# An extra GpSimd addition behind each scatter, and TensorE products in four column groups

## The chip, the cores and the metric

The kernel runs on one core of a Trainium2 chip. A core has five engines with instruction streams of their own: TensorE (PE in the profile; its weight loads are PEld), VectorE (DVE), ScalarE (ACT), GpSimd (POOL) and SyncE (SP, which here only issues DMAs); a q behind the name (SPq) is that engine's sequencer. They meet through semaphores. TensorE writes to PSUM, a memory of eight banks of 2 KB per partition; VectorE and ScalarE read it from there. The metric is the device time of one execution in microseconds, of which the median of several runs is taken. The profiled execution is one more, and all rows below are from it.

## The reference

All inputs are float32. Attention with `B, H, S, D = 2, 8, 768, 64` in which a query sees only keys of its own cluster, then an ELU feed-forward layer, then a routed mixture of experts:

```python
q_assign = np.argmax(np.einsum('bhsd,hcd->bhsc', q_n, c_n), axis=-1)   # 16 centroids a head
k_assign = np.argmax(np.einsum('bhsd,hcd->bhsc', k_n, c_n), axis=-1)
mask = q_assign[:, :, :, None] == k_assign[:, :, None, :]
scores = np.where(mask, scale * np.matmul(q, k.transpose(0, 1, 3, 2)), -1e9)
attn_out = softmax(scores) @ v
x = attn_out.transpose(0, 2, 1, 3).reshape(B * S, H * D)               # 1536 x 512
h = x @ w_in; g = np.where(h > 0, h, np.exp(np.minimum(h, 0)) - 1)     # 512 -> 2048
x = g @ w_out                                                          # 2048 -> 512
do_compute = x @ w_skip > 0                                            # a token is skipped or routed
logits = x @ w_gate; e_idx = argmax(logits); gate_w = softmax(logits)[e_idx]   # 8 experts
out = x + where(do_compute, gate_w * (relu(x @ w1[e_idx]) @ w2[e_idx]), 0)     # 512 -> 1024 -> 512
```

## The kernel before

The two batches are treated differently. Batch 0 is "dense": four units n = 0 to 3, each a pair of heads, compute all 768 x 768 scores of each head with the mask folded into the product as extra rows. Batch 1 is "sorted": for the pairs j = 0 to 3 (`NSORT = 4`) the rows of q, k and v are written to DRAM in the order of their cluster, and only pieces of rows that can share a cluster are multiplied.

**Order.** Inside the attention and the feed-forward layer no scheduler orders anything: `ORDER` (L49) is one flat list of steps, written out by hand, each `name:n`. The steps are issued one after the other, each step sends its instructions to the engines that it uses, and every engine works through its own part of the list in that order. The routing of the last block has a list of its own, `TAIL` (L35), in which `h` steps are products of the feed-forward layer, `T` turns a token tile, `L` takes its gate logits, `C` chooses, `R` ranks, `F` fills, `x` fetches.

**Dense unit.** `turn`, `turn_head` and `turn_rest` (L349 to L377) transpose q and k and split them into a high and a low part in float32r (a form of float32 that TensorE multiplies in one pass), kept as `T[n][nm, "H"]` and `["L"]`. Then the clusters: `similar` (L399) multiplies the centroids with q and k; per half of 384 tokens there are three float32r products (high x high, high x low, low x high) for q and three for k, which fill partitions 0 to 63 of a PSUM bank through the zero-padded weights `cwH` and `cwL`; `similar_out` (L403) copies a half to SBUF, and `turn_back` (L408) makes six transposes of 64 x 128, so that tokens lie on partitions. `largest` (L425), `less_largest` (L429, on GpSimd), `candidates`, `first_of_them` and `one_hot` make the argmax one-hot, `turn_one_hot` and `mask_rows` make mask rows of it, and `move` (L463, SyncE) puts rows into place by DMA. `v_rest` (L490, GpSimd) splits v. Then for twelve pieces s of each unit: `scores` (L498), `peak` (L504, VectorE), `expo` (L511, ScalarE), `flip` (L519, three TensorE transposes a half into PSUM), `head` (L531, ScalarE copies the transposed half to float32r), `rest` (L537, VectorE subtracts that copy), `pv`, `pv_low`, `pv_sum` (L550 to L567, products with v).

**Sorting, spread among the dense units' steps.** For pair j: `sort_turn` and `sort_raw` (L703, L708) transpose q and k of batch 1; `sort_similar` (L716) makes twelve float32 products with the 32 columns of `cwF` as the moving side, which land with tokens on partitions. `sort_max` to `sort_index` (L755) compute each token's row, `idx`. `sort_zero` (L688, L689) clears the DRAM buffers with DMAs of SyncE. `sort_scatter` (L770) sends one indirect DMA from GpSimd for each pair j, chunk c of 128 tokens and r (q or k and v, of head 0 or 1):

```python
store = self.nc.gpsimd.indirect_dma_start(
    dst[2 * j + h], bass.IndirectOffsetOnAxis(ap=self.idx[:, j, 4 * c + r:4 * c + r + 1], axis=0),
    self.sort_rows(j, c // 3)[:, c % 3, lo:hi], None, bounds_check=1023, oob_is_err=False)
```

That is 24 for each pair and 96 in all (steps `sc0a` to `sc5d`). They stand in the list alone between other engines' steps, so on GpSimd they mostly follow each other.

**Sorted rows.** `rows_load` (L794) reads the sorted rows back, two heads of a pair at a time, and `rows_turn` to `rows_divide` (L801 to L856; L836 is the transpose) do attention on 16 pieces. `gather` (L868) fetches results in token order with 48 indirect DMAs of GpSimd, which stand among the rounding steps of the weights (`round64`, L1202 to L1223; its last operation, L1223, is a GpSimd addition) and `w_low` (L1249, GpSimd).

**Feed-forward and routing.** `ffn_h` (L1269) and `ffn_second` or `second_ops` (L1308, L1325) multiply in two blocks of 768 tokens, 16 steps of 128 columns each. Routing takes 12 token tiles: `route` turns a tile (L1445), makes four float32 products of the turned tile with 16 columns of gate weights `wgs` (L1453), copies the logits (L1455), then `choose` (from L1457). For the first block this stands beside the second block's feed-forward (`route_beside`), for the last in `TAIL`. Then each of eight experts computes its tokens (L1675 to L1768).

Of the kernel before, what the change touches and what calls it, by code (L numbers as in the profile page):

```python
# [10 lines left out]
F32 = mybir.dt.float32  # L11
F32R = mybir.dt.float32r
# [22 lines left out]
TAIL = ("h3 h3 h3 T0 T2 h3 L0 T1 h5 L2 L1 T3 h5 C0 h4 h4 R0 h4 h4 x- T4 h5 L3 L4 C3 h5 x0 T5 R3 x2 L5 x4 F0 C5 R5 N5 x3 x1 x5 F5 F3").split()  # L35
# [22 lines left out]
    simq1:1 exp5:0 rest3b:0 simk1:1 peak6:0 head4a:0 sT1:1 flip4b:0 rest4a:0 scores7a:0 suk1:0 loadv:0 head4b:0 flip5a:0
    scores7b:0 sek1:0 back:1 exp6:0 rest4b:0 sv:1 flip5b:0 peak7:0 sload0:1 scores8a:0 mx:1 scores8b:0 head5a:0 ssim0:0 eqsub:1
    ssim1:0 pv1a:0 rest5a:0 pv1c:0 peak8:0 pv1b:0 flip6a:0 pv1d:0 head5b:0 exp7:0 scores9b:0 first:1 exp8:0 rest5b:0 scores10a:0  # L60
    least:1 smx:0 vtH:1 flip6b:0 sone:0 head6a:0 pvlow1:0 scum:0 srank:0 pvsum1:0 pv2a:0 rest6a:0 flip7a:0 pv2c:0 equal:1 pv2b:0
    head7a:0 vtL:1 pv2d:0 moveT0:1 scores9a:0 sidx:0 rows:1 head6b:0 rest6b:0 flip7b:0 sc2c:0 rest7a:0 pvlow2:0 peak9:0 oT:1
    flip8a:0 loadqk:1 head7b:0 pvsum2:0 rest7b:0 exp9:0 scores10b:0 turnq0:2 peak10:0 pv3a:0 pv3b:0 pv3c:0 scores11b:0 sc3b:0
    scores11a:0 sc4b:0 THq0:2 TLq0:2 flip8b:0 turnq1:2 sc0d:0 head8a:0 sc5a:0 rest8a:0 exp10:0 moveO0:1 flip9a:0 head8b:0
    scores0a:1 peak11:0 THq1:2 head9a:0 scores0b:1 rest8b:0 pv3d:0 TLq1:2 flip9b:0 rest9a:0 exp11:0 turnk0:2 flip10a:0 head9b:0
    rest9b:0 pvlow3:0 pvsum3:0 scores1b:1 scores1a:1 head10a:0 flip10b:0 sc0a:0 pv4a:0 rest10a:0 flip11a:0 THk0:2 peak0:1
    sload1:1 sc3a:0 TLk0:2 pv4b:0 pv4c:0 head10b:0 rest10b:0 head11a:0 exp0:1 pv4d:0 suq0:1 seq0:1 flip11b:0 scores2a:1 sc2d:0
    sc1b:0 pvlow4:0 rest11a:0 flip0a:1 turnk1:2 peak1:1 pvsum4:0 head11b:0 THk1:2 exp1:1 rest11b:0 TLk1:2 scores2b:1 pv5a:0
    peak2:1 invert:0 head0a:1 pv5b:0 flip0b:1 suq1:1 zero:1 pv5c:0 scores3a:1 seq1:1 sc4d:0 scores3b:1 simq0:2 head0b:1 rest0a:1
    exp2:1 sc2a:0 simk0:2 sc1a:0 flip1a:1 rest0b:1 peak3:1 flip1b:1 scores4a:1 sT0:2 head1a:1 scores4b:1 rest1a:1 moveT1:1  # L70
    suk0:1 exp3:1 sc5b:0 pv5d:0 flip2a:1 sc1c:0 peak4:1 moveO1:1 sek0:1 loadv:3 head1b:1 scores5a:1 sc5c:0 simq1:2 sc0b:0 smem:0
    simk1:2 head2a:1 exp4:1 rest1b:1 scores5b:1 flip2b:1 scores6b:1 sT1:2 head2b:1 rest2a:1 loadv:1 pvlow5:0 suk1:1 flip3a:1
    peak5:1 scores6a:1 rest2b:1 sc1d:0 sek1:1 flip3b:1 back:2 sumT:0 exp5:1 scores7a:1 pvsum5:0 sc2b:0 head3a:1 peak6:1 rest3a:1
# [91 lines left out]
class _Core:  # L165
# [26 lines left out]
    def first_loads(self):  # L192
# [1778 lines left out]
```

## Time and profile before

| | us |
|---|---|
| median of three runs (747.60 to 751.81) | 749.87 |
| the profiled execution | 748.56 |
| its span, first to last instruction | 746.8 |
| TensorE busy (85% of the span) | 635.4 |
| VectorE busy (58%) | 431.6 |
| ScalarE busy (53%) | 392.9 |
| GpSimd busy (36%) | 271.7 |

Busy shares are means over a span in which several stages follow each other: the dense units until about 260 us, then the sorted rows, the feed-forward layer until about 605 us, routing and experts. "remote" as the releaser of a wait means that the trace shows no instruction of this core whose end set the semaphore just then; the chain of waits calls the same thing "another core or an unknown queue". A `<-issue` is time in which an engine waited for nothing that the trace shows.

### The profile page before, as it was taken

What the parts mean: (1) busy time and instruction counts of PE and PEld (TensorE: products, weight loads), DVE (VectorE), ACT (ScalarE), POOL (GpSimd) and SP (SyncE); (2) the same over time, 40 slices, a digit from 0 to 9 for tenths busy, and PEclk for the clock granted to TensorE, in tenths of its full rate; (3) what the DMA queues carried; (4) which work ended last, traced back from release to release, by engine and by line L of the source; (5) the groups of instructions that cost most, each with busy time, mean ns of one, the idle gap of its engine ahead of it and who ended that gap; (6) DMA issues with size and microseconds to landing.
All of it is one profiled execution on the core that took longest, in us unless ns stands there. A gap on an engine that the chain in (4) does not pass through costs nothing.

```text
span 746.8 us, 11604 instructions
## 1 busy us (share of the span) xinstructions
PE 635.4 (85%) x3988; PEld 576.0 (77%) x3988; DVE 431.6 (58%) x982; ACT 392.9 (53%) x850; POOL 271.7 (36%) x289
## 2 busy tenths in 40 slices
PE   5991892874772399999999999999999999999996
PEld 3881882773662399888989889999998988999995
DVE  6680790872660398999698775333245545135663
ACT  4761770852641398776776765544544622124552
POOL 3247067047057302865664352323223203121101
PEclk9795896897695599999999999999999999999999
DMA  7877064576331039666654553642421027989960
GB/s 174 208 172 195 14 156 112 129 159 165 91 90 37 22 101 251 183 178 199 204 180 154 165 161 101 254 169 61 165 57 57 14 110 266 384 291 319 335 231 18
DMA packets 99957, 118.30 MB, mean 158 GB/s; under 512 B 47553, under 2 KB 68209, under 8 KB 99888
## 3 DMA queue, kind: packets, MB, share of 16 engines
q1 hardware_dynamic: 92080, 106.70, 47.4%
q0 software_dynamic: 6096, 10.34, 4.3%
q8 instruction: 33, 0.54, 0.3%
q10 hardware_dynamic: 1712, 0.43, 0.3%
q14 instruction: 36, 0.29, 0.1%
HBM read 80.17 MB, written 27.80 MB: 145 GB/s over the span
## 4 chain that ended last, share of the span: by engine, by line
PE 65%; DVE 11%; another core or an unknown queue 11%; ACT 6%; issue 3%; DMA 1%; SPq 0%; POOL 0%; POOLq 0%; ACTq 0%; DVEq 0%
PE ps_p L1269 7%; PE ps_v L1269 6%; PE ps_t L1720 5%; PE ps_t L519 4%; PE ps_p L1735 4%; PE ps_v L1735 4%; PE ps_v L550 4%; PE ps_sB L1308 3%; PE ps_sA L1308 3%; PE ps_t L1308 3%; PE ps_sA L498 2%; PE ps_sB L498 2%; PE ps_sA L1325 2%; DVE cv_b L1217 1%
## 5 line engine op out<-in xcount | busy, mean ns | idle before, releaser
L519 PE MATMUL ps_t<-ident,pe 128*128 128x128 f32 x288 | 53.5, 307 | 59.9 <-issue 30.4
L519 PEld LDWEIGHTS ps_t<-ident,pe 128*128 128x128 f32 x288 | 38.6, 159 | 66.8 <-issue 32.8
L531 ACT ACTIVATE ptH<-ps_t 128x384 fp32r<-128x384 f32 x96 | 46.0, 491 | 82.5 <-remote 59.0
L537 DVE TENSOR_TENSOR ptL<-ps_t,ptH 128x384 fp32r<-128x384 f32 x96 | 52.1, 551 | 58.9 <-ACT ptH L531 45.7
L868 POOL DMA_INDIRECT og<-od,idx x48 | 51.2, 1066 | 55.2 <-ACT rp L830 27.8
L1223 POOL TENSOR_TENSOR r<-cv_b,cv_t 128x512 int32<-128x512 int32 x32 | 42.9, 1341 | 47.5 <-DVE cv_b L1217 19.7
L550 PE MATMUL ps_v<-ptH,vt 128*128 128x256 f32 x144 | 44.0, 328 | 14.6 <-issue 8.6
L1269 PE MATMUL ps_p<-xH,w1H 128*128 128x384 f32 x128 | 44.3, 346 | 1.9 <-DVE gL L1297 1.5
L1768 POOL DMA_INDIRECT out_dram<-o,dest x10 | 11.0, 1104 | 93.4 <-DVE o L1766 92.8
L1293 DVE SCALAR_TENSOR_TENSOR ps_p<-e,ps_p 128x384 f32<-128x384 f32 x32 | 17.9, 560 | 45.1 <-ACT e L1291 45.1
L550 PEld LDWEIGHTS ps_v<-ptH,vt 128*128 128x128 f32 x144 | 30.7, 215 | 16.6 <-issue 9.3
L1269 PE MATMUL ps_v<-xH,w1H 128*128 128x384 f32 x124 | 42.0, 339 | 1.3 <-DVE gL L1297 1.3
L1269 PE MATMUL ps_p<-xL,w1H 128*128 128x384 f32 x128 | 43.0, 336 | 0.0
L550 PE MATMUL ps_v<-ptL,vt 128*128 128x256 f32 x144 | 41.5, 312 | 0.3 <-DVE ptL L537 0.3
L1269 PE MATMUL ps_v<-xL,w1H 128*128 128x384 f32 x124 | 41.6, 335 | 0.0
L1249 POOL TENSOR_TENSOR w2L<-r,w2H 128x512 fp32r<-128x512 f32 x12 | 15.3, 1279 | 71.5 <-PE ps_t L1308 57.4
L1289 ACT ACTIVATE e<-ps_p 128x384 f32<-128x384 f32 x32 | 15.7, 490 | 40.7 <-PE ps_p L1269 40.7
L770 POOL DMA_INDIRECT kvs<-rowsH,idx x24 | 23.8, 990 | 33.8 <-DVE idx L755 23.1
L1735 PE MATMUL ps_p<-xs,ew 128*128 128x128 f32 (+2 forms) x256 | 35.4, 280 | 0.5 <-ACT xs L1683 0.5
L1735 PEld LDWEIGHTS ps_p<-xs,ew 128*128 128x128 f32 x256 | 33.7, 191 | 2.3 <-ACT xs L1683 0.6
L1735 PEld LDWEIGHTS ps_v<-xs,ew 128*128 128x128 f32 x256 | 33.7, 191 | 1.8
L1735 PE MATMUL ps_v<-xs,ew 128*128 128x128 f32 (+2 forms) x256 | 35.0, 279 | 0.0
(491 smaller groups left out, 2006.7 us busy)
## 6 DMA issues: line engine op xcount, KB each, us to landing
ew<-in_moe_w_dram SPq DMA_DIRECT2D x32, 1024.0 KB
d<-in_moe_w_in_dram SPq DMA_DIRECT2D x16, 512.0 KB
d<-in_moe_w_out_dram SPq DMA_DIRECT2D x16, 512.0 KB
wf_d<-r SPq DMA_DIRECT2D x16, 512.0 KB
r<-wf_d SPq DMA_DIRECT2D x16, 512.0 KB
zk<-kvs SPq DMA_DIRECT2D x8, 520.0 KB
KA<-kH SPq DMA_DIRECT2D x16, 192.0 KB
kvs<-zeros SPq DMA_DIRECT2D x8, 325.0 KB
```

Of the source, the lines that this page charges most:

```text
L498: self.nc.tensor.matmul(self.sc[u][:, half, 0:384], lhsT=d["Q" + a][0:rows, c * 128:c * 128 + 128], rhs=d["K" + a][0:rows, half * 384:half ...
L519: self.nc.tensor.transpose(ps[:, 0, j * 128:j * 128 + 128], self.pe[u][:, half, j * 128:j * 128 + 128], self.ident)
L531: self.nc.scalar.activation(self.split(u, half)[0], self.tp[u, half][:, 0, 0:384].rearrange("p (c q) -> p c q", c=3), AF.Copy)
L537: self.nc.vector.tensor_tensor(l, self.tp.pop((u, half))[:, 0, 0:384].rearrange("p (c q) -> p c q", c=3), h.bitcast(F32), ALU.subtract)
L550: self.nc.tensor.matmul(self.vp[n, j], lhsT=self.vt[n][:, j // NG, c, :], rhs=t, start=(part == 0 and i == 0), stop=(part == 3 and i == 2 ...
L770: store = self.nc.gpsimd.indirect_dma_start(dst[2 * j + h], bass.IndirectOffsetOnAxis(ap=self.idx[:, j, 4 * c + r:4 * c + r + 1], axis=0), ...
L868: self.nc.gpsimd.indirect_dma_start(self.og[j][:, c, h, :], None, self.o_d[i], bass.IndirectOffsetOnAxis(ap=self.idx[:, j, 4 * c + h:4 * c ...
L1223: G.tensor_tensor(r[:, j * 512:j * 512 + 512].bitcast(I32), b, self.cvt.pop((f, j)), ALU.add)
L1269: self.nc.tensor.matmul(ps, lhsT=w[:, c, :], rhs=x[:, c, :], start=(i == 0), stop=(i == 11))
L1308: self.nc.tensor.matmul(self.y[bl][part][t], lhsT=a[:, t * 128:t * 128 + 128], rhs=w, start=(f == 0 and i == 0), stop=(f == NF - 1 and i = ...
L1720: PE.matmul(y[0][0:W], lhsT=a, rhs=b, start=(f == 0 and i == 0), stop=(f == NF - 1 and i == 2))
L1735: PE.matmul(ps[:, 0:W], lhsT=w1[:, c, i * 128:i * 128 + 128], rhs=xs[:, c, 0:W], start=(c == 0), stop=(c == 3))
```

## The change

There are five parts. Behind each of the 96 scatters GpSimd adds a tile `idle` of 128 x 96 elements to itself; nothing reads the tile otherwise.

The centroid products of a dense unit are now four products of 384 columns in float32, (half 0, half 1) x (q, k), each with the 32 columns of `cwF` as weights and each writing its own 32 partitions of one PSUM bank; the high and the low part of q and k are multiplied one after the other and summed, so there are eight instructions in the code. One copy of 128 x 384 and three transposes of 128 x 128 follow. `cwH` and `cwL` are gone. The sorted pairs get the same form, four float32 products, a copy (`sTT`) and three transposes (`sback`). Since the columns come out in another order, the index tile is addressed through `group` and `index`.

The gate logits are four products in the same manner: for each 128 of the 512 features the 32 columns of weights stay and the tile's 128 tokens move, into 32 partitions of their own; a copy, one transpose and a sum over the four parts follow, done just after the next tile's products (`back`), or by `B` in `TAIL`. The tile that stands alone (`nt == 1`) keeps the old form.

`second_ops` names its operands through indices; the instructions are the same. `ORDER` is written anew: 1890 steps in place of 1902. The scatters stand at much the same places among the dense steps, the fills `zero:2` and `zero:3` stand 14 and 20 exponentials earlier, `bload1` and `bload2` earlier too. `TAIL` has `B0` and `B3`, with `h5` and `h4` steps ahead of `B0`.

```diff
@@ -32,7 +32,8 @@
-TAIL = ("h3 h3 h3 T0 T2 h3 L0 T1 h5 L2 L1 T3 h5 C0 h4 h4 R0 h4 h4 x- T4 h5 L3 L4 C3 h5 x0 T5 R3 x2 L5 x4 F0 C5 R5 N5 x3 x1 x5 F5 F3").split()
+TAIL = ("h3 h3 h3 T0 T2 h3 L0 T1 h5 L2 h5 L1 T3 h4 B0 C0 h4 h4 h4 x- R0 T4 h5 L3 h5 L4 x0 B3 C3 T5 x2 L5 R3 x4 "
+        "F0 C5 R5 N5 x3 x1 x5 F5 F3").split()
@@ -47,119 +48,118 @@
 ORDER = """
-    turnq0:0 THq0:0 turnq1:0 TLq0:0 THq1:0 turnk0:0 TLq1:0 THk0:0 turnk1:0 TLk0:0 THk1:0 TLk1:0 simq0:0 simk0:0 loadqk:0 sT0:0
...
+    turnq0:0 THq0:0 turnq1:0 TLq0:0 THq1:0 turnk0:0 TLq1:0 THk0:0 turnk1:0 TLk0:0 THk1:0 TLk1:0 loadqk:0 sim:0 sT:0 back:0 sv:0
+    mx:0 eqsub:0 turnq0:1 rawq0:1 first:0 THq0:1 turnq1:1 TLq0:1 least:0 rawq1:1 THq1:1 equal:0 TLq1:1 rows:0 moveT0:0 moveO0:0
...
@@ -390,22 +384,23 @@
-    def similar(self, n, nm, half):
-
-        p, cs, o = n % (self.H // 2), slice(half * 384, half * 384 + 384), 32 if nm == "q" else 0
-        if nm == "q":
-            self.sim[n, half] = self.bank_p()
-        for j, (w, x) in enumerate(((self.cwH, "H"), (self.cwH, "L"), (self.cwL, "H"))):
-            self.nc.tensor.matmul(self.sim[n, half][0:64, 0:384], lhsT=w[:, p, o:o + 64], rhs=self.T[n][nm, x][:, cs],
-                                  start=(nm == "q" and j == 0), stop=(nm == "k" and j == 2))
-
-    def similar_out(self, n, half):
-        self.nc.scalar.activation(self.rows[0:64, half * 384:half * 384 + 384], self.sim.pop((n, half))[0:64, 0:384], AF.Copy)
+    def similar(self, n):
+
+        ps, p, T = self.bank_p(), n % (self.H // 2), self.T[n]
+        self.sim[n] = ps
+        for x in "HL":
+            for i, (half, nm) in enumerate(itertools.product(range(2), "qk")):
+                self.nc.tensor.matmul(ps[32 * i:32 * i + 32, 0:384], lhsT=self.cwF[:, p, :],
+                                      rhs=T[nm, x][:, half * 384:half * 384 + 384].bitcast(F32), start=(x == "H"), stop=(x == "L"))
+
+    def similar_out(self, n):
+        self.simT = self.sort_tile("sT", [128, 384], F32)
+        self.nc.scalar.activation(self.simT, self.sim.pop(n)[:, 0:384], AF.Copy)
         ps = self.back[n] = self.bank_p()
-        for c in range(self.NC):
-            self.nc.tensor.transpose(ps[:, c * 64:c * 64 + 64], self.rows[0:64, c * 128:c * 128 + 128], self.ident[0:64, 0:64])
+        for c in range(3):
+            self.nc.tensor.transpose(ps[:, c * 128:c * 128 + 128], self.simT[:, c * 128:c * 128 + 128], self.ident)
@@ -654,6 +647,8 @@
         G.memset(self.zeros, 0.0)
+        self.idle = d.tile([128, 96], F32, name="idle")
+        G.memset(self.idle, 0.0)
@@ -707,14 +702,21 @@
-    def sort_similar(self, j, half):
-        if half == 0:
-            self.ssim = self.bank_p()
-        for c in range(3 * half, 3 * half + 3):
-            for i, nm in enumerate("qk"):
-                o = c * 64 + 32 * i
-                self.nc.tensor.matmul(self.ssim[:, o:o + 32], lhsT=self.sT[j, nm][:, c * 128:c * 128 + 128],
-                                      rhs=self.cwF[:, j, :], start=True, stop=True)
+    def sort_similar(self, j):
+
+        ps = self.ssims = self.bank_p()
+        for i, (half, nm) in enumerate(itertools.product(range(2), "qk")):
+            self.nc.tensor.matmul(ps[32 * i:32 * i + 32, 0:384], lhsT=self.cwF[:, j, :],
+                                  rhs=self.sT[j, nm][:, half * 384:half * 384 + 384], start=True, stop=True)
+
+    def sort_similar_out(self, j):
+        self.ssT = self.sort_tile("sT", [128, 384], F32)
+        self.nc.scalar.copy(self.ssT, self.ssims[:, 0:384])
+
+    def sort_similar_back(self, j):
+        self.ssim = self.bank_p()
+        for c in range(3):
+            self.nc.tensor.transpose(self.ssim[:, c * 128:c * 128 + 128], self.ssT[:, c * 128:c * 128 + 128], self.ident)
@@ -764,12 +766,20 @@
+    def group(self, c):
+        return c % 3 * 8 + c // 3 * 4
+
+    def index(self, j, c, r):
+        g = self.group(c) + r
+        return self.idx[:, j, g:g + 1]
+
     def sort_scatter(self, j, c, r):
         store = self.nc.gpsimd.indirect_dma_start(
-            dst[2 * j + h], bass.IndirectOffsetOnAxis(ap=self.idx[:, j, 4 * c + r:4 * c + r + 1], axis=0),
+            dst[2 * j + h], bass.IndirectOffsetOnAxis(ap=self.index(j, c, r), axis=0),
             self.sort_rows(j, c // 3)[:, c % 3, lo:hi], None, bounds_check=1023, oob_is_err=False)
+        self.nc.gpsimd.tensor_tensor(self.idle, self.idle, self.idle, ALU.add)
         before = self.stores.setdefault((kv, 2 * j + h), [])
@@ -866,7 +876,7 @@
         self.nc.gpsimd.indirect_dma_start(self.og[j][:, c, h, :], None, self.o_d[i],
-                                          bass.IndirectOffsetOnAxis(ap=self.idx[:, j, 4 * c + h:4 * c + h + 1], axis=0),
+                                          bass.IndirectOffsetOnAxis(ap=self.index(j, c, h), axis=0),
                                           bounds_check=1023, oob_is_err=False)
@@ -1447,12 +1457,32 @@
         def logits(t):
-            lp = bank()[:, 0:16]
+            lp = bank()
             x2T = held.pop(t)
+            if nt == 1:
+                for j in range(4):
+                    PE.matmul(lp[:, 0:16], lhsT=x2T[:, j * 128:j * 128 + 128], rhs=self.wgs[:, j, 0:16],
+                              start=(j == 0), stop=(j == 3))
+                V.tensor_copy(lg[:, t, :], lp[:, 0:16])
+                return
             for j in range(4):
-                PE.matmul(lp, lhsT=x2T[:, j * 128:j * 128 + 128], rhs=self.wgs[:, j, :],
-                          start=(j == 0), stop=(j == 3))
-            V.tensor_copy(lg[:, t, :], lp)
+                PE.matmul(lp[32 * j:32 * j + 32, 0:128], lhsT=self.wgs[:, j, :], rhs=x2T[:, j * 128:j * 128 + 128],
+                          start=True, stop=True)
+            before = back(lp)
+            lgT = fw.tile([128, 128], F32, tag="lgT", bufs=2, name="lgT")
+            (S.copy if b else V.tensor_copy)(lgT, lp[:, 0:128])
+            held["back"] = t, lgT
+            before()
+
+        def back(ps=None):
+            if "back" not in held:
+                return lambda: None
+            t, lgT = held.pop("back")
+            if ps is None:
+                ps = bank()
+            PE.transpose(ps[:, 128:256], lgT, self.ident)
+            add = lambda: V.tensor_reduce(lg[:, t, :], ps[:, 128:256].rearrange("p (j e) -> p e j", j=4)[:, 0:16, :], axis=AX.X, op=ALU.add)
+            return add
```

## Rows read from the trace of the kernel before

**Rows 1.** Busy us by window: PE, PEld, DVE, ACT, POOL; clock, DMA; last their sum.

```profile
100.00:150.00 50.00, 32.93 (x220) 29.10 (x219) 29.32 (x59) 25.47 (x58) 21.27 (x22) 0.80 0.50 130
...
200.00:250.00 50.00, 23.28 (x158) 20.41 (x155) 19.46 (x40) 15.20 (x34) 29.31 (x31) 0.72 0.17 54
...
300.00:350.00 50.00, 46.91 (x298) 42.97 (x296) 46.46 (x90) 36.53 (x80) 34.49 (x31) 1.00 0.60 179
...
sum 200.00, PE 118.78 PEld 106.09 DVE 100.18 ACT 88.29 POOL 96.58; mean PE 29.70 PEld 26.52 DVE 25.05 ACT 22.07 POOL 24.15
```

**Rows 2.** Chain that ended last, by line (share of the span).

```profile
by line: another core or an unknown queue 10.7%; PE ps_p L1269 6.6%; PE ps_v L1269 6.5%; PE ps_t L1720 4.6%; PE ps_t L519 4.3%; PE ps_p L1735 4.0%; PE ps_v L1735 4.0%; PE ps_v L550 3.7%; issue 3.2%; PE ps_sB L1308 3.2%; PE ps_sA L1308 3.2%;
```

**Rows 3.** Waits (engine, line, waited for: us, times, longest), ScalarE and SyncE.

```profile
ACT ptH L531 <- remote: 59.0, 11, 14.3
...
SPq L463 <- PE ps_sB L498: 29.1, 3, 23.0
```

**Rows 4.** Timeline (start, us, engine, line, operation, idle before) of the first run of scatters.

```profile
49.07 1.16 POOL L770 DMA_INDIRECT kvs<-rowsH,idx  x1 [4.00 <-DMA natq<-in_q_dram]
...
61.73 0.90 PE L519 MATMUL ps_t<-ident,pe 128*128 128x128 f32 x3 [0.54 <-issue]
...
75.56 0.49 ACT L531 ACTIVATE ptH<-ps_t 128x384 fp32r<-128x384 f32 x1 [13.60 <-remote]
```

**Rows 5.** Busy time in 13 stretches without TensorE, VectorE and ScalarE, one and sum.

```profile
217.40:218.80 1.40, 0.00 (x0) 0.00 (x0) 0.00 (x0) 0.00 (x0) 1.10 (x2) 1.00 1.14 298
...
sum 58.36, PE 0.00 PEld 0.00 DVE 0.00 ACT 0.00 POOL 39.15; mean PE 0.00 PEld 0.00 DVE 0.00 ACT 0.00 POOL 3.01
```

**Rows 6.** Timeline, single rows: SyncE, GpSimd's last scatters, ScalarE's last exponential.

```profile
139.15 0.99 SPq L689 DMA_DIRECT2D kvs<-zeros  x1
...
211.56 0.97 POOL L770 DMA_INDIRECT kvs<-rowsH,idx  x1 [23.11 <-DVE idx L755]
...
249.85 0.97 POOL L770 DMA_INDIRECT qs<-rowsL,idx  x1 [0.30 <-issue]
...
261.63 0.91 ACT L511 ACTIVATE pe<-ps_sB,st 128x768 f32<-128x768 f32 x1
```

**Rows 7.** Timeline of GpSimd among the gathers.

```profile
307.01 1.30 POOL L868 DMA_INDIRECT og<-od,idx  x1 [0.30 <-issue]
308.34 1.28 POOL L1223 TENSOR_TENSOR r<-cv_b,cv_t 128x512 int32<-128x512 int32 x1
309.78 1.02 POOL L868 DMA_INDIRECT og<-od,idx  x1 [0.16 <-issue]
```

**Rows 8.** Busy time in two windows without a run of scatters.

```profile
76.00:112.00 36.00, 34.28 (x245) 31.78 (x246) 32.17 (x65) 27.56 (x63) 11.68 (x12) 0.91 0.37 88
303.00:320.00 17.00, 15.47 (x126) 14.81 (x124) 15.65 (x42) 13.17 (x35) 13.64 (x13) 1.00 0.53 154
```

**Rows 9.** Groups of instructions: xcount | busy, mean ns of one | idle before.

```profile
L490 POOL TENSOR_TENSOR vt<-natv,vt 128x768 fp32r<-128x768 f32 x4 | 7.3, 1831 | 7.9 <-ACT vt L486 7.9
...
L377 POOL TENSOR_TENSOR kL<-raw,kH 128x384 fp32r<-128x384 f32 x2 | 2.0, 1002 | 0.2
...
L770 POOL DMA_INDIRECT kvs<-rowsL,idx x24 | 23.5, 979 | 9.2 <-issue 6.7 <-DVE idx L755 2.5
...
L716 PE MATMUL ps_p<-cwF,sT 128*128 128x32 f32 x96 | 11.2, 271 | 0.0
...
L836 PE MATMUL ps_t<-ident,rp 128*128 128x128 f32 x64 | 9.9, 277 | 1.2 <-issue 1.2
```

**Rows 10.** Pieces of the chain that ended last (start, us, what).

```profile
85.97 1.06 PE ps_p L399 x6
...
201.26 1.26 PE ps_p L716 x12
...
204.14 0.36 PE ps_t L519 x3
...
604.00 0.89 PE ps_v L1453 x8
```

More of the change, by code (lines that the diff above doesn't have):

```diff
@@ L58 @@
[L58 to L61, printed above, removed]
@@ new lines @@
+    rest2a:1 sek1:1 sc2d:0 flip3a:1 exp4:1 head2b:1 loadqk:2 pv0b:1 back:2 head3a:1 sumT:0 pv0c:1 peak5:1 sv:2 exp5:1 scores6b:1
+    rest2b:1 rest3a:1 scores6a:1 flip4a:1 invrow:0 zero:3 head4a:1 pv0d:1 mx:2 flip3b:1 scores7a:1 sc0d:0 scores7b:1 peak6:1
+    rest4a:1 flip5a:1 head3b:1 pvlow0:1 head5a:1 rest3b:1 sc4c:0 flip4b:1 eqsub:2 head4b:1 ssim:1 sTT:1 pvsum0:1 sback:1 peak7:1
+    first:2 rest5a:1 exp6:1 exp7:1 vtH:2 sc3b:0 least:2 rest4b:1 scores8a:1 invdma:0 smx:1 sc5b:0 scores8b:1 flip5b:1 moveT0:2
@@ L1041, in redo_experts @@
             for c in range(4):
-                PE.matmul(ps, lhsT=xT[:, c, i * 128:i * 128 + 128], rhs=self.wgs[:, c, :], start=(c == 0), stop=(c == 3))
+                PE.matmul(ps, lhsT=xT[:, c, i * 128:i * 128 + 128], rhs=self.wgs[:, c, 0:16], start=(c == 0), stop=(c == 3))
             V.tensor_copy(lg[:, i], ps)
@@ L1084, in sort_steps @@
             put(f"sload{half}", self.sort_load, half)
-            put(f"ssim{half}", self.sort_similar, half)
             for nm in "qk":
@@ L1320, in second_ops @@
         bl, f = divmod(k, NF)
-        (w2H, w2L), g = self.w_sp[k, 1], [self.gs[k, part] for part in range(2)]
+        w = self.w_sp[k, 1]
         def product(part, t, i):
-            a, w = ((g[part][0], w2H), (g[part][1], w2H), (g[part][0], w2L))[i]
-            self.nc.tensor.matmul(self.y[bl][part][t], lhsT=a[:, t * 128:t * 128 + 128], rhs=w,
+            a = self.gs[k, part][i % 2]
+            self.nc.tensor.matmul(self.y[bl][part][t], lhsT=a[:, t * 128:t * 128 + 128], rhs=w[i // 2],
                                   start=(f == 0 and i == 0), stop=(f == NF - 1 and i == 2))
@@ L1499, in route @@
         return ([lambda t=t: copy(t) for t in range(nt)], [lambda t=t: turn(t) for t in range(nt)],
-                [lambda t=t: logits(t) for t in range(nt)], choose, rank, fill)
+                [lambda t=t: logits(t) for t in range(nt)], lambda ps=None: back(ps)(), choose, rank, fill)
     def first_fetch(self):
@@ L1551, in route_beside @@
         yield
-        for _, turn, logits, choose, rank, fill in halves:
+        for _, turn, logits, back, choose, rank, fill in halves:
             for i in range(3):
@@ L1557, in route_beside @@
                 yield
+            back(self.ps("p")[:, 0, :])
             choose()
@@ L1577, in route_last @@
         for c0, ys in ((0, y[0]), (3, y[1][0:2]), (5, y[1][2:3])):
-            copy, turn, logits, choose, rank, fill = self.route(b, c0, ys, bank)
+            copy, turn, logits, back, choose, rank, fill = self.route(b, c0, ys, bank)
             for i in range(len(ys)):
-                steps["c", c0 + i], steps["T", c0 + i], steps["L", c0 + i] = copy[i], turn[i], logits[i]
+                for x, f in zip("cTL", (copy, turn, logits)):
+                    steps[x, c0 + i] = f[i]
+            steps["B", c0] = back
             steps["C", c0], steps["R", c0], steps["F", c0] = choose, rank, fill
```

237 lines of the change are left out of this document (114 added, 123 removed).

## The prediction

> **What bounds the kernel now.** I read the page's busy shares first, then the chain that ended last, then busy time by 50 us stretch. By the busy shares (the table above) TensorE comes first, but it is so by stages: 23 to 33 us of each 50 us from 50 to 250 us, at a granted clock of 0.72 to 0.80, and 47 of 50 us at 300 to 350, at 1.00, and more after that [rows 1]. From 300 us on the kernel is bound by TensorE; before 260 us it is bound by something else. The chain says by what: 10.7% of the span, 80 us, stands at "another core or an unknown queue" [rows 2]. There is no other core, so this is a wait whose release the trace cannot name.
>
> The waits name the places: ScalarE, at the copies of TensorE's results out of PSUM (L531), waits 59.0 us in 11 pieces for "remote" [rows 3]. In the timeline of the first such place TensorE issues three transposes at 61.73 us; ScalarE's copy of them starts at 75.56 us, after 13.60 us of waiting. GpSimd meanwhile issues scatter after scatter, 19 in a row from 49.07 us, 1.28 us apart, and the copy goes on some two microseconds after the last [rows 4]. I cut out 13 stretches of this kind, all from 63 to 253 us: together 58.4 us, in which TensorE, VectorE and ScalarE do nothing at all and GpSimd is busy 39.2 us [rows 5]. I know no data dependence of L531 on a scatter in the code. So I read it as a hold-up that scatters cause in how TensorE's completion reaches the other engines.
>
> It needs a run of scatters. The last of the four runs starts at 211.56 us [rows 6], and the engines first stop at 217.4 us [rows 5], after five scatters; the second and third run show the same, the first stops them later. The gathers at 298 to 320 us are indirect DMAs too, about as long, but GpSimd has other work between them: four gathers, an addition, three gathers, an addition [rows 7]. In 303 to 320 us TensorE is busy 15.5 of 17 us, although GpSimd is busy 13.6 us with ten gathers and three additions [rows 8]. That speaks for an ordinary instruction between indirect DMAs ending the hold-up, or for the larger mean distance (1.7 us for each gather in place of 1.28); the trace cannot tell these apart.
>
> **The change part by part.** *The additions.* 96 of 128x96 elements, one behind each scatter. GpSimd's additions or subtractions take 1831 ns at 768 elements and 1002 at 384 [rows 9]; from 384 to 768 that is 2.16 ns per element and 0.17 us fixed, so an estimate of 0.38 us at 96 (bounds: 0.17 and the 1.00 us row). A scatter then follows an addition after some 0.15 us, as the gather at 309.78 us does, and an addition follows an indirect DMA between 0.98 us (a scatter's length, [rows 9]) and 1.33 us after its start (307.01 to 308.34 us, [rows 7]). So one scatter and its addition take 0.98 + 0.38 + 0.15 = 1.51 us, at most 1.86; I take 1.51, nearest to L770's own length. GpSimd's own chain from the first scatter is then 49 + 96 x 1.51 + 5 (two `vt` and two `eq`) + 5 for index waits = 204 us, where it ends at 250.8 us now [rows 6].
>
> *What it removes, if the runs are broken.* 58.4 us in which nothing computes. Dense attention's last exponential would come at 261.6 - 58.4 = 203 us [rows 6]. The stretch 76 to 112 us without long stops shows what is late next: TensorE 34.3, VectorE 32.2 and GpSimd 11.7 of 36 us [rows 8]; the engines' own work fills it, so nothing more is gained than the stops, and GpSimd's 204 us lies beside it. The sorted rows need the last scatters only for heads 6 and 7, and by the flat order heads 0 to 5 come first, so GpSimd's end is covered by some 40 us of other rows. If that cover is gone, its end sets the stage. I leave 8 us for short stops that stay, and count **-50 us**.
>
> *Centroid products.* Per head pair and unit 12 products of 384 columns go, 6 in 1.06 us at full clock: 2.1 us [rows 10]. In their place are 8 fp32 products of 384 columns. An fp32 product shows as two matmuls (L716 has 96 for 48 in the code; [rows 9]), so 16. No row shows one of 384: bounds are 0.177 us (one of L399) and three times a 128-column fp32 matmul, 3 x 0.111 = 0.334 us (0.89 us for eight, [rows 10]). One after another they would take up to 5.3 us, four side by side at 0.177 us 0.7 us. No row shows column groups either; I take 0.334 us and four side by side, since the four write different partitions: 1.34 us, -0.8 us per unit (bounds -1.4 and +3.2). The sorted products were 24 matmuls, 12 in 1.26 us twice; 8 of 384 columns take 0.67 (0.35 to 2.7) plus three transposes at 0.36 us: -1.5 us (-1.8 to +0.5), and a ScalarE copy of some 0.49 us (as L531, [rows 4]) that was not there, offset in the dense half by one copy in place of two. Six transposes back become three. Over four units and four sorts: -9 us of TensorE work, bounds -13 to +15. VectorE is nearly as busy as TensorE there, so I count half: **-4 us**.
>
> *Gate logits.* Eleven of twelve token tiles: 8 matmuls in 0.89 us [rows 10] become 8 in column groups, 0.22 us side by side, plus one transpose of 0.11: -0.5 each, or +0.1 one after another. Six lie in the second feed-forward half, where TensorE is the bound, and five in the routing tail on the chain, where a copy and a sum are added ahead of the choice; other products stand there to cover them (the order moves `h5` and `h4` ahead of `B0`), worth about 1 us if they don't. **-4 us**, bounds -6 to +2.
>
> *Moved steps.* The order carries the same scatters by progress; the zero fills of pairs 2 and 3 move forward on SP by 14 and 20 exponentials: four issues each of up to 0.99 us [rows 6] ahead of the moves of the next unit. SP's moves wait up to 23.0 us for TensorE there [rows 3], which hides 4 us; without that cover it is 4 us per pair. The reordered operands in the second product are the same instructions. **0** (0 to +8).
>
> The sum: -50 - 4 - 4 = -58 us. The profiled execution took 748.56 us (span 746.8 and 1.8 around it): 690.6. The median of the runs is 749.87 us, 1.3 above: **692 us**.
>
> **A rule of the Trainium skill.** The trace shows no product that uses one column group among several: every L399 row writes 64 columns at place 0. The Trainium skill (TensorEngine Tiling (Array Packing), Tiling Modes, Key Properties) says that tiles load and multiply in parallel, but that changing the tiling mode drains TensorE; no run here shows it. If a drain is what a lone 128-column transpose takes beyond its share, 277 - 111 = 0.17 us [rows 9, 10], then 19 places with two changes each cost an estimate of 6 us, and the sum would be 698 us.
>
> **The rivals.**
> *C, slower: the hold-up lasts as long as scatters keep coming.* Then an addition only makes each run longer. For it: the first long stop ends after the last scatter of its run (75.56 us, [rows 4]). Against it: the gathers. Price: 96 x (1.51 - 1.28) = 22 us more GpSimd time; as GpSimd's end sets this stage's end, 748.6 + 22 - 4 = **766 us**. It decides if stops of all three engines in the new trace still sum to over 60 us.
> *B: GpSimd becomes the bound.* At 1.86 us its chain ends at 49 + 179 + 10 = 238 us; `eq` and `vt` of the next unit, and then gathers and weight additions, wait behind scatters in its queue. GpSimd's end then comes only 13 us sooner, the compute up to 45: 703 to 735, I take **720 us**.
> *D: the column groups run one after another.* +15 in place of -9 on TensorE, which is then the bound in the dense stage, and +1 in place of -4: 692 + 15 + 4 + 5 = **716 us**.
> *E: the additions do nothing and cost nothing* (hidden in the stops): **746 us**.
>
> **How the numbers follow.** The forecast 0.52, with 665 to 712 as its own range (58 us of stops and all of TensorE's savings, or half of the stops left). B 0.16, C 0.16, D 0.12, E 0.04. Range 655 to 750: its low end adds TensorE's higher clock (118.8 us of work at 0.72 to 0.80 in 50 to 250 us, [rows 1], of which some 10 us could come back) and the lower bounds of the products; C lies outside. About 0.5% can be told from no change here: faster 0.80, same 0.04, slower 0.16.
>
> **What would show it.** Right: no stretch over 3 us before 260 us in which TensorE, VectorE and ScalarE are all idle while scatters run; L531 waits for "remote" under 15 us; a scatter every 1.5 us; granted clock over 0.85 from 50 to 200 us; the sorted rows' first scores before 215 us. Products wrong: new L399 matmuls that start over 0.3 us apart, against four that start together. The prediction is wrong if scatters still stop the engines with an addition between them, or if GpSimd is busy throughout and others wait for it by name.

## The result, and the profile after

The changed kernel takes 682.41 us (median of 4 runs, 670.82 to 685.12) where the kernel before takes 749.44: a ratio of 0.9004, interval 0.8952 to 0.9056. Medians here are of all runs, ratios leave out runs that count as slow (over 1.5% above the fastest run of the same kernel; here the two of 685 us), so a ratio can lie a little below the quotient of its medians, which is 0.911 here. The forecast was 692. The profiled execution took 685.12 us (span 683.4) and is thus at the long end of its runs; the second profiled execution of the changed kernel (after_again, 675.62 us) is in the table below.

The busy time by window, in the columns of [rows 1]:

```profile
100.00:150.00 50.00, 41.81 (x278) 34.57 (x279) 40.06 (x80) 34.70 (x78) 37.15 (x54) 0.93 0.59 143
...
200.00:250.00 50.00, 45.22 (x386) 42.69 (x385) 42.01 (x115) 41.15 (x94) 38.06 (x47) 1.00 0.71 207
sum 200.00, PE 169.44 PEld 146.24 DVE 161.42 ACT 145.61 POOL 149.46; mean PE 42.36 PEld 36.56 DVE 40.36 ACT 36.40 POOL 37.37
```

From 50 to 250 us TensorE does 169.4 us of work where it did 118.8, at a granted clock of 0.90 to 1.00 in its four windows instead of 0.72 to 0.80. The chain of waits that ended last no longer has the unknown queue that stood first in [rows 2]:

```profile
by line: PE ps_p L1279 7.2%; PE ps_v L1279 7.0%; PE ps_t L1753 5.0%; PE ps_p L1768 4.4%; PE ps_v L1768 4.3%; PE ps_sB L1318 3.5%; PE ps_sA L1318 3.4%; PE ps_t L1318 3.4%; PE ps_sA L1335 1.5%; PE ps_t L1335 1.5%; PE ps_sB L1335 1.4%; PE ps_s
```

ScalarE's copy, the line that waited 59.0 us for "remote" [rows 3], is now L526. In its group (mean ns of one, then idle before it by what ended it) only TensorE is left as a large releaser:

```profile
L526 ACT ACTIVATE ptH<-ps_t 128x384 fp32r<-128x384 f32 x96 | 45.8, 491 | 24.8 <-PE ps_t L514 13.9 <-issue 2.5 <-PE ps_v L545 2.4
```

GpSimd's timeline shows the rhythm: an addition of 0.36 us, and a scatter every 1.54 us (1.51 was worked out, from [rows 7, 9]):

```profile
92.14 0.99 POOL L779 DMA_INDIRECT kvs<-rowsH,idx  x1 [0.17 <-issue]
93.16 0.36 POOL L782 TENSOR_TENSOR idle<-idle 128x96 f32<-128x96 f32 x1
93.68 0.99 POOL L779 DMA_INDIRECT qs<-rowsH,idx  x1 [0.16 <-issue]
```

And the last exponential of the dense units starts 70.7 us earlier than in [rows 6]:

```profile
190.89 0.91 ACT L506 ACTIVATE pe<-ps_sB,st 128x768 f32<-128x768 f32 x1
```

For what follows, a kernel's trace is cut in three: up to the start of the last dense exponential, from there to the end of the last second product of the feed-forward layer, and from there to the end of the span. "Stops" are all stretches of over 0.6 us between 1 and 270 us in which TensorE, VectorE and ScalarE all do nothing; for the kernel before this count gives 61.7 us, with some short ones beside the 58.4 of [rows 5].

| kernel (chip) | us, ratio to before on its chip [95%] | stops | dense | middle | end |
|---|---|---|---|---|---|
| before | 749.44 | 61.7 | 261.6 | 351.9 | 133.2 |
| changed | 682.41, 0.9004 [0.8952, 0.9056] | 2.0 | 190.9 | 354.3 | 138.2 |
| changed, again: after_again (2) | 677.17, 0.8968 [0.8881, 0.9055] | 0 | 181.6 | 353.7 | 138.7 |
| adds_only (2) | 673.16, 0.8961 [0.8895, 0.9027] | 1.9 | 177.9 | 360.3 | 133.5 |
| no_adds (2) | 755.37, 1.0055 [1.0030, 1.0079] | 52.8 | 263.1 | 350.6 | 138.1 |
| short_adds (2) | 741.79, 0.9870 [0.9815, 0.9925] | 35.9 | 248.7 | 353.4 | 133.2 |
| adds_48 (0) | 724.01, 0.9652 [0.9601, 0.9704] | 14.7 | 217.0 | 366.4 | 134.1 |
| adds_paired (0) | 685.51, 0.9131 [0.9085, 0.9177] | 9.6 | 176.5 | 371.2 | 133.3 |
| old_logits (0) | 677.96, 0.8983 [0.8923, 0.9043] | 0 | 178.2 | 358.2 | 134.8 |
| old_products (0) | 685.62, 0.9081 [0.9028, 0.9134] | 0.6 | 193.7 | 353.4 | 138.0 |
| before_again (13) | 645.11, 0.9996 [0.9981, 1.0010] | 0 | 158.5 | 351.0 | 132.7 |
| adds_only_again (4) | 663.89, 1.0307 [1.0279, 1.0335] | 1.1 | 168.3 | 359.3 | 132.6 |
| old_order (4) | 666.33, 1.0319 [1.0298, 1.0341] | 0 | 171.8 | 362.3 | 132.7 |
| adds_double (4) | 721.41, 1.1190 [1.1168, 1.1211] | 45.4 | 197.8 | 389.3 | 132.6 |

Chips go by the number noted with each run; that of the first measurement is not noted. The kernel before took 751.47 us on chip 2, 751.21 on chip 0, 644.65 on chip 4 and 645.77 on chip 13. That is the main thing the experiments found, and it came last.

### The profile page after: what moved, and what is told of

Read it like the earlier page. It is cut to its first block, busy times and chain, and to the rows that moved or that the text cites. A ratio compares the mean times of both kernels' runs of the same rounds, so it can differ in the third digit from the quotient of the medians.

```text
span 683.4 us, 11659 instructions
## 1 busy us (share of the span) xinstructions
PE 624.5 (91%) x3951; PEld 550.3 (81%) x3951; DVE 440.3 (64%) x984; ACT 395.3 (58%) x853; POOL 313.9 (46%) x386
## 4 chain that ended last, share of the span: by engine, by line
PE 50%; DVE 2%; issue 1%; POOL 0%; POOLq 0%; ACT 0%
PE ps_p L1279 7%; PE ps_v L1279 7%; PE ps_t L1753 5%; PE ps_p L1768 4%; PE ps_v L1768 4%; PE ps_sB L1318 3%; PE ps_sA L1318 3%; PE ps_t L1318 3%; PE ps_sA L1335 2%; PE ps_t L1335 1%; PE ps_sB L1335 1%; PE ps_sA L1756 1%; PE ps_sB L1756 1%; PE ps_sA L1565 1%; PE ps_p L1455 1%
## 5 line engine op out<-in xcount | busy, mean ns | idle before, releaser
L514 PE MATMUL ps_t<-ident,pe 128*128 128x128 f32 x288 | 51.0, 294 | 15.7 <-issue 6.9
L878 POOL DMA_INDIRECT og<-od,idx x48 | 54.0, 1126 | 14.4 <-issue 11.7
L526 ACT ACTIVATE ptH<-ps_t 128x384 fp32r<-128x384 f32 x96 | 45.8, 491 | 24.8 <-PE ps_t L514 13.9
L514 PEld LDWEIGHTS ps_t<-ident,pe 128*128 128x128 f32 x288 | 35.4, 150 | 25.3 <-issue 12.9
L545 PE MATMUL ps_v<-ptH,vt 128*128 128x256 f32 x144 | 41.9, 312 | 1.6 <-DVE xr L562 0.8
L782 POOL TENSOR_TENSOR idle<-idle 128x96 f32<-128x96 f32 x96 | 36.2, 377 | 2.1
L1301 ACT ACTIVATE e<-e 128x384 f32<-128x384 f32 x64 | 33.6, 525 | 1.8
```

The costliest lines, as they stand in the source:

```text
L514: self.nc.tensor.transpose(ps[:, 0, j * 128:j * 128 + 128], self.pe[u][:, half, j * 128:j * 128 + 128], self.ident)
L526: self.nc.scalar.activation(self.split(u, half)[0], self.tp[u, half][:, 0, 0:384].rearrange("p (c q) -> p c q", c=3), AF.Copy)
L545: self.nc.tensor.matmul(self.vp[n, j], lhsT=self.vt[n][:, j // NG, c, :], rhs=t, start=(part == 0 and i == 0), stop=(part == 3 and i == 2 ...
L782: self.nc.gpsimd.tensor_tensor(self.idle, self.idle, self.idle, ALU.add)
L878: self.nc.gpsimd.indirect_dma_start(self.og[j][:, c, h, :], None, self.o_d[i], bass.IndirectOffsetOnAxis(ap=self.index(j, c, h), axis=0), ...
L1301: S.activation(e, e, AF.Exp, scale=-1.0)
```

## The experiments

**The parts taken apart.** The additions alone on the kernel before (adds_only), and everything but the additions (no_adds):

```diff
             self.sort_rows(j, c // 3)[:, c % 3, lo:hi], None, bounds_check=1023, oob_is_err=False)
+        self.nc.gpsimd.tensor_tensor(self.idle, self.idle, self.idle, ALU.add)   # adds_only
```

> The kernel before with the 96 additions of 128x96 behind the scatters and nothing else. Theory 1 (the additions end the hold-up, the other parts bring some 8 us): the stops of TensorE, VectorE and ScalarE before 260 us sum to under 6 us instead of 58.4, ScalarE's wait for remote at L531 falls under 10 us, and the time is 680 to 697 us. Rival 2 (the new flat order brings most of it): stops over 40 us, 735 to 755 us. Rival 3 (the additions and the new order only work together, since GpSimd's longer queue delays eq and vt of the next unit in the old order): stops gone, but GpSimd named as the releaser of waits instead, 700 to 725 us.

> The changed kernel without the 96 additions; column groups, logits and the new order stay. Theory 1: the stops come back, over 40 us in sum before 260 us, and the time is 735 to 747 us. Rival 2 (the new order brings most of it): 680 to 700 us, stops under 15 us.

> The changed kernel as it is, on the same chip as the three others, to have a base for them: 670 to 686 us, as in its first four runs.

Theory 1 holds in its main part: with the additions the stops go (1.9 us), without them they stay (52.8 us). Both times lie outside its ranges, 673.16 below 680 and 755.37 above 747, because the additions bring more than it had and the other parts bring nothing. The additions alone bring 78 us; its busy sum from 50 to 250 us and its last exponential:

```profile
sum 200.00, PE 181.18 PEld 162.61 DVE 165.85 ACT 149.31 POOL 159.07; mean PE 45.29 PEld 40.65 DVE 41.46 ACT 37.33 POOL 39.77
...
177.89 0.91 ACT L511 ACTIVATE pe<-ps_sB,st 128x768 f32<-128x768 f32 x1
```

Without them the rest of the change costs 0.3 to 0.8% on this chip, and the waits for "remote" are back, some at other lines than before:

```profile
ACT ptH L526 <- remote: 27.9, 3, 12.7
DVE st L499 <- remote: 26.6, 4, 17.2
```

**What ends the hold-up.** The prediction left open whether an ordinary instruction or the distance does it. Shorter additions, and the same 96 additions two at a time behind every second scatter:

```diff
-        self.idle = d.tile([128, 96], F32, name="idle")
+        self.idle = d.tile([128, 1], F32, name="idle")      # short_adds; adds_48: [128, 48]
```

```diff
+        if self.scattered % 2 == 0:                          # adds_paired
+            for _ in range(2):
+                self.nc.gpsimd.tensor_tensor(self.idle, self.idle, self.idle, ALU.add)
```

> The kernel before with an addition of 128x1 elements behind each scatter, so that a scatter follows the one before it after about 1.3 us, as it did without additions. Theory 1a (any ordinary GpSimd instruction between two scatters ends the hold-up): stops under 6 us, within 4 us of the kernel with additions of 96 elements, 676 to 697 us. Theory 1b (the distance between scatters matters): stops over 40 us stay, 740 to 752 us.

> The kernel before with additions of 128x48 elements. A scatter then follows the one before it after some 1.46 us; it was 1.28 us without additions (749 us), 1.37 us with 128x1 (742 us) and 1.54 us with 128x96 (673 us). Theory A (the distance counts, the more the better, without an edge): on the line between the last two, 700 to 712 us. Theory B (an edge below 1.46 us): 670 to 680 us, stops under 6 us. Theory C (an edge above 1.46 us): 735 to 745 us, stops over 25 us.

> The kernel before with the same 96 additions of 128x96, but two of them behind every second scatter and none behind the others: gaps of some 1.28 and 1.9 us by turns, mean about 1.58 us. Theory D (the mean rate of scatters counts): stops under 8 us, 672 to 686 us. Rival (every gap counts): half of the stops stay, 700 to 735 us.

GpSimd's timeline and ScalarE's wait for "remote", first of short_adds, then of adds_48:

```profile
108.27 0.98 POOL L772 DMA_INDIRECT kvs<-rowsH,idx  x1 [0.16 <-issue]
109.28 0.20 POOL L775 TENSOR_TENSOR idle<-idle 128x1 f32<-128x1 f32 x1
109.64 0.99 POOL L772 DMA_INDIRECT qs<-rowsL,idx  x1 [0.16 <-issue]
...
ACT ptH L531 <- remote: 52.1, 13, 12.2
```

```profile
106.58 0.98 POOL L772 DMA_INDIRECT kvs<-rowsH,idx  x1 [0.17 <-issue]
107.59 0.27 POOL L775 TENSOR_TENSOR idle<-idle 128x48 f32<-128x48 f32 x1
108.03 0.98 POOL L772 DMA_INDIRECT kvs<-rowsH,idx  x1 [0.17 <-issue]
...
ACT ptH L531 <- remote: 8.3, 7, 3.1
```

An instruction between two scatters is not enough: with one of 0.20 us the wait is still 52.1 us, with one of 0.27 us 8.3. short_adds came out near theory 1b (741.79 us; 35.9 us of stops, where it had over 40). From 1.28 to 1.37, 1.45 and 1.54 us between scatters the ratio goes 1, 0.987, 0.965, 0.896, so no theory met adds_48: it lies above the line of A and at no edge. The dense part alone goes more evenly, 261.6, 248.7, 217.0, 177.9 us; adds_48 also loses 14.5 us in its middle part. In adds_paired the scatters come by turns 1.29 and 2.18 us after the one before:

```profile
111.23 0.99 POOL L772 DMA_INDIRECT kvs<-rowsH,idx  x1 [0.36 <-issue]
112.52 0.98 POOL L772 DMA_INDIRECT qs<-rowsL,idx  x1 [0.30 <-issue]
113.51 0.82 POOL L778 TENSOR_TENSOR idle<-idle 128x96 f32<-128x96 f32 x2
114.70 0.99 POOL L772 DMA_INDIRECT kvs<-rowsL,idx  x1 [0.36 <-issue]
```

Its dense part is as short as with single additions, 176.5 us, so a gap of 1.29 us does no harm when a long one follows. Of its 9.6 us of stops (theory D had under 8) 7.4 end with a wait for GpSimd by name, for the step `eq` of the argmax, and are no hold-up:

```profile
DVE eq L434 <- POOL eq L429: 13.4, 2, 6.8
```

What makes it slower is the middle, 10.9 us longer than in adds_only: GpSimd's last scatter starts at 223.5 us instead of 212.2. So not every short gap counts, as theory D had it. That it is the mean rate (a scatter each 1.74 us here) is not shown beyond that: a rule by which no more than two scatters may follow each other closely would give the same.

**The other parts.** In old_logits the gate logits and `TAIL` are as before, in old_products `similar` and `sort_similar` make the old products at the new places of the order:

```diff
-            if nt == 1:
+            if True:                                         # old_logits, with the old TAIL
```

```diff
     def similar(self, n):                                    # old_products
+        for half in range(2):
+            for nm in "qk":
+                self.similar_half(n, nm, half)               # as before, with cwH and cwL
```

> The changed kernel with the gate logits of all tiles in the old form and the old order of the routing tail; additions, column groups of the centroids and the new flat order stay. Theory (the new logits and the new tail order lengthen the routing tail: from the last second product to the end it takes 138.6 us in the changed kernel and 133.9 us in the kernel with the additions alone): 5 us less there, so 670 to 675 us where the changed kernel takes 677. Rival (the prediction's step: the new logits save 4 us of TensorE): 679 to 684 us.

> The changed kernel with the centroid products of the dense units and of the sorted pairs in the old form (twelve and 24 matmuls, six transposes), at the places of the new ones in the new flat order. The prediction's step (the groups save 9 us of TensorE work, half of it on the path): 680 to 685 us. Rival (the stage is set by GpSimd's scatters and by VectorE, TensorE's saving is not on the path): 674 to 679 us, the last exponential at about the same time.

The end does get shorter with the old logits (134.8 us, against 138.0 to 138.7 in the four traces with the new ones); the whole time, 677.96 us and between the two expectations, does not show it, because the dense part differs by 9 us between two executions of the changed kernel alone (190.9 and 181.6). old_products is slower by 1.1 to 1.3% than old_logits and after_again, with intervals that overlap, so its 685.62 us, just above the 680 to 685 of the prediction's step, does not decide. Whether the new products gain in the old order was tried next, with old logits too (the steps that change, for unit and pair 1):

```diff
-    simq0:1 simk0:1 sT0:1 simq1:1 simk1:1 sT1:1
+    sim:1 sT:1
...
-    ssim0:1 ssim1:1
+    ssim:1 sTT:1
...
-    smx:1
+    sback:1 smx:1
```

> The additions and the new centroid products, but in the flat order of before (each product, copy and transposes at the place of the old ones, sTT behind the second half's products and sback ahead of the maximum), with the old gate logits and the old tail. Theory P (the new products save some 8 us in any order, as they do in the new one: 685.6 against 677 us): 662 to 668 us, the fastest of all. Rival (the old products only suffered from the places that the new order gave them, and the additions alone are the whole gain): 671 to 677 us.

> The kernel with the additions alone once more, on the same chip as its neighbours, as their base: 670 to 678 us.

> The kernel before with two additions of 128x96 behind every scatter: a scatter every 1.9 us or so. Theory B (GpSimd's own work becomes the bound: 96 x 0.35 us more in its queue, and the sorted rows wait for the last scatters): 685 to 705 us, the last exponential not later than 180 us. Rival (at 1.54 us engines are still held up in part, more distance gains more): 655 to 668 us.

These three met chip 4, where the kernel before takes 644.65 us. All three are slower than it. The times expected for them were worked out on the other chips and don't hold here; old_order lies in theory P's range only for that reason. old_order and adds_only_again can't be told apart (1.0319 and 1.0307), so in the old order and on this chip the new products gain nothing that could be seen. The additions cost 19 us there: the last exponential of adds_only_again starts at

```profile
168.31 0.91 ACT L511 ACTIVATE pe<-ps_sB,st 128x768 f32<-128x768 f32 x1
```

In adds_double (two additions behind every scatter, a scatter each 2.15 us) GpSimd is the bound, as theory B had it, though dearer (721.41 us for at most 705, the last exponential at 197.8 us for at most 180): the argmax step `eq` (L429) of the next unit stands behind the scatters in GpSimd's queue, and VectorE waits for it by name, with all else behind that:

```profile
90.83 0.84 POOL L429 TENSOR_TENSOR eq<-eq,mx 128x384 f32<-128x384 f32 x1
91.71 0.56 DVE L434 SCALAR_TENSOR_TENSOR eq<-eq,iota_neg 128x384 f32<-128x384 f32 x1 [15.64 <-POOL eq L429]
...
DVE eq L434 <- POOL eq L429: 32.1, 2, 16.5
```

These two stops, 26.7 of its 45.4 us, are no hold-up: their releaser is in the trace. The other two, 13.9 and 4.8 us, stand at 225 to 253 us, and the trace does not name who ends them. The first fits sorted rows that are read back late, while GpSimd still scatters: SyncE issues the load of `zk` at 233.95 us, and TensorE starts on it at 239.01. Of the second no more is shown.

```profile
233.95 0.61 SPq L798 DMA_DIRECT2D zk<-kvs  x1
...
239.01 1.03 PE L811 MATMUL ps_v<-ident,zk 128*66 128x128 f32 x4 [18.18 <-issue]
```

**The kernel before on a chip without the hold-up.**

> The kernel before once more, for a trace of it on whichever chip it meets. Its time was 749 to 751 us on three chips and 644.65 us on the fourth. Theory H (the hold-up belongs to some chips, and the whole difference of 105 us lies in the dense stage): on a chip where it takes about 645 us, the stops sum to under 6 us with scatters still 1.28 us apart, no wait for remote at L531 over 5 us, and the last exponential starts at about 158 us (261.6 now, less the 104 us); on a chip where it takes about 750 us, 50 to 65 us of stops as in the first trace. Rival (the fourth chip is faster in every stage): 645 us with the stages after the dense one shorter by 14% too.

It met chip 13, and theory H holds: windows, two scatters in a row and the last exponential, and ScalarE's copy:

```profile
100.00:150.00 50.00, 49.72 (x384) 45.84 (x382) 47.84 (x103) 41.81 (x97) 34.91 (x36) 1.00 0.80 204
...
200.00:250.00 50.00, 46.99 (x287) 42.65 (x286) 47.44 (x91) 35.71 (x78) 32.80 (x30) 1.00 0.64 185
sum 200.00, PE 195.18 PEld 180.19 DVE 187.22 ACT 166.65 POOL 141.45; mean PE 48.79 PEld 45.05 DVE 46.80 ACT 41.66 POOL 35.36
```

```profile
60.81 0.97 POOL L770 DMA_INDIRECT kvs<-rowsL,idx  x1 [0.30 <-issue]
62.09 0.97 POOL L770 DMA_INDIRECT qs<-rowsH,idx  x1 [0.30 <-issue]
...
158.47 0.91 ACT L511 ACTIVATE pe<-ps_sB,st 128x768 f32<-128x768 f32 x1
```

```profile
L531 ACT ACTIVATE ptH<-ps_t 128x384 fp32r<-128x384 f32 x96 | 45.8, 492 | 12.4 <-PE ps_t L519 11.6
```

The scatters are as dense as ever, 1.28 us apart, that copy no longer waits for "remote", TensorE works 49.7 of 50 us at a clock of 1.00, and the last exponential starts 103.1 us earlier than in [rows 6]. Middle and end are as long as before to within 1 us, so the rival falls. For the dense stage the two traces of the one program give this, the same 1051 TensorE instructions in both, first with the hold-up and then without:

```profile
0.00:261.60 261.60, 164.69 (x1051) 145.84 (x1052) 140.42 (x298) 124.76 (x274) 112.87 (x155) 0.78 0.50 123
0.00:158.50 158.50, 145.61 (x1051) 131.26 (x1052) 137.89 (x298) 123.35 (x275) 94.19 (x135) 0.97 0.80 197
```

In 84 of the 103 us TensorE stands still (96.9 us against 12.9), in 62 of them VectorE and ScalarE as well; the other 19 are its own instructions taking longer, at a granted clock of 0.78 instead of 0.97.

## Why the prediction was right, and where it was not

The time was right, and the largest step was right in kind: scatters hold up the completion of TensorE's work, and 96 additions end nearly all of that. The signs that were to show it came: no stop over 1.00 us, no wait of L526 for "remote", a scatter every 1.54 us, the clock at 0.90 to 1.00, the sorted rows' first scores at 190 us. That the total came within 10 us of the measured time is in part luck, since two errors had opposite signs. By its steps:

- **The additions, "-50 us", were mis-sized: they measured -78** (adds_only; 751.47 to 673.16). I priced the stretches in which all three engines stand still. The hold-up costs 103 us of the dense part (261.6 against 158.5 on chip 13): beside the stops it is 22 us in which TensorE stands still while VectorE or ScalarE works, and 19 us of a lower clock, which I had put only into the low end of the range, with 10. The additions win back 83.7 us and lose 8.4 in the middle part. By the traces of the old order that part grows with how long scatters go on after the last dense exponential starts: the last scatter comes 27, 34, 47 and 68 us after it in before_again, adds_only, adds_paired and adds_double, and the middle takes 351.0, 360.3, 371.2 and 389.3 us. I had counted GpSimd's end as covered by 40 us of other rows. I had it at 204 us; the last scatter starts at 212.2 (adds_only) and 225.8 (changed). The 250.8 us that I set against it were also misread, since one scatter of the kernel before stands behind the first gather:

```profile
280.00 1.02 POOL L770 DMA_INDIRECT qs<-rowsH,idx  x1 [0.31 <-issue]
```

- **Of the two readings of the gathers [rows 7, 8], "an ordinary instruction between indirect DMAs" falls:** with an addition of 0.20 us behind each scatter 35.9 us of stops stay. The distance counts, and on some chips not even that: 1.28 us is harmless there.
- **The price of an addition** (0.38 us, a pair each 1.51) measured 377 ns and 1.54 us.
- **The centroid products, "-4 us"**: the price was right. In TensorE's timeline of the changed kernel four products start within 0.03 us, a round of four takes 0.33 us, and four rounds 1.3 us, where I had 1.34:

```profile
126.75 0.51 PE L393 MATMUL ps_p<-qH,cwF 128*32 128x384 f32 x1
126.76 0.51 PE L393 MATMUL ps_p<-kH,cwF 128*32 128x384 f32 x1
...
127.10 0.49 PE L393 MATMUL ps_p<-qH,cwF 128*32 128x384 f32 x1
...
127.42 0.49 PE L393 MATMUL ps_p<-qL,cwF 128*32 128x384 f32 x1
...
127.74 0.49 PE L393 MATMUL ps_p<-qL,cwF 128*32 128x384 f32 x1
...
128.18 0.39 PE L545 MATMUL ps_v<-ptH,vt 128*128 128x256 f32 x1
```

It brought nothing that could be shown: without the hold-up old_order is no faster than adds_only_again. The Trainium skill (TensorEngine Tiling (Array Packing), Key Properties) has a drain at a change of the tiling mode. The trace agrees in kind: the next product starts 0.42 us after the last round, 0.09 more than a round takes, here and at four other such places; I had estimated 0.17.
- **The gate logits, "-4 us", had the wrong sign in the end part**: 138.0 to 138.7 us with them, 134.8 with the old ones in the new order, 133.2 in the kernel before. The six tiles beside the feed-forward layer were not measured by themselves. TensorE's timeline in the end part, then a window:

```profile
550.48 0.71 PE L1565 MATMUL ps_sA<-sel,xL 128*128 128x128 f32 x4 [1.45 <-DVE sel L1561]
...
556.71 1.06 PE L1565 MATMUL ps_sA<-sel,xL 128*128 128x128 f32 x4
...
552.50:560.00 7.50, 7.50 (x49) 7.32 (x50) 4.78 (x31) 0.53 (x2) 0.00 (x0) 0.61 0.25 65
```

and the same of the kernel before:

```profile
620.86 0.61 PE L1535 MATMUL ps_sA<-sel,xL 128*128 128x128 f32 x4
...
618.50:623.50 5.00, 4.73 (x47) 4.55 (x45) 4.22 (x33) 0.43 (x2) 0.00 (x0) 1.00 0.07 25
```

The choice now comes later behind a copy, a transpose and a sum; TensorE pauses 1.45 us for VectorE's `sel`, and from 552.5 to 560 us its granted clock is 0.61 (at half, 1.2 GHz, until 558.4) and the fetching products take 1.06 us for 0.61. The clock is not the logits' doing alone, though. In old_logits it falls as well, behind a pause of 0.27 us that the kernel before has too, at a clock of 1.00:

```profile
541.87 0.17 PE L1645 MATMUL ps_t<-acc,ones 128*128 128x8 bf16 x1 [0.27 <-DVE acc L1501]
...
543.53 1.06 PE L1564 MATMUL ps_sA<-sel,xH 128*128 128x128 f32 x4
```

From the last second product to the first product of an expert it takes 9.4 us in the nine traces with the old logits and the old order, 11.0 in old_logits, 12.9 in old_products, and 14.4 in the other three with the new logits; the clock is at half for 0, 3.4, 3.4 and 6.8 us of it. So the pause and the added work cost some 1.7 us, near my "about 1 us if they don't", and the clock, which I had left out, 1.7 or 3.4 us (an estimate: half of the time at half clock). What makes it fall is not shown.
- **The moved steps, "0"**, were not measured by themselves. Together, what is not the additions sums to +4 us (no_adds, 1.0055) where I had -8.

So two errors of 28 and 12 us had opposite signs. And a loss, as rival C forecast it with a chance of 0.16, is what happens on chip 4: there the additions only lengthen GpSimd's work and cost 19 us where I had priced 22, though not for the reason given (no wait for "remote" stands out in that trace, and 1.1 us of stops).

What stays open: why the hold-up is there on chips 0 and 2 (and on that of the first measurement) and not on 4 and 13. The runs of one chip fall together in time, so it could be a state of the machine as well as of the chip. Nor is its mechanism shown. The number of bytes or rows of a scatter was not varied, and neither the changed kernel nor the additions were run on chip 13.

## What to carry to other kernels

Price a stall from what the stage would take without it, not from the sum of its visible gaps: the lower clock and the stretches in which only some engines stood still were another 41 us beside 62. Before a workaround is built, look whether the stall is there on another chip; here the same program took about 750 us on some and 645 on others, and the workaround that wins 10% on the one loses 3% on the other. No version that was run beats both kernels on both kinds of chip: with the hold-up it is the additions alone or the whole change, which can't be told apart, without it the kernel before (the whole change was not run there).

## What the runs showed of the hardware that was not expected

Indirect DMAs of GpSimd issued back to back can hold up the semaphores of other engines on one chip and not on another, with the same instructions 1.28 us apart. The raw events of the kernel before show it from 240.5 to 252.6 us: the scatters' own semaphores come 0.2 to 0.7 us after the last packet of each, but TensorE's, whose last product there ends at 240.50 us, come at 246.23 and 252.53 us, and each time a waiting instruction starts within 0.1 us (VectorE's L504, ScalarE's L531). Of the 656 TensorE instructions that raise a semaphore, 51 end more than 1 us before its next recorded rise, by up to 12.9 us; in before_again 3 do, by up to 1.4 us (in either trace a record can be missing).

Spacing by 0.26 us more takes nearly all of it away, by 0.09 us only a part. Some of it stays even so: adds_only on chip 2 has 37 such instructions, by up to 3.9 us, and a dense part of 177.9 us; the same kernel on chip 4 has 4, by up to 1.8 us, and 168.3 us.
